# A state-space layer and a long convolution on one core: the parameter rows issued from one queue, and the first blocks' small work in another order

## The chip, the cores and the metric

The kernel runs on one core of a Trainium2 chip. The metric is the device time of one execution in microseconds (us). The kernel before took 198.16 us (median of three runs, 197.69 to 199.36).

## The reference, cut to what matters

Two independent layers work on 2048 rows of 640 channels in bf16, and their outputs are joined along the channels.

```
# A: diagonal complex state space, P = D = 640
dt = exp(log_dt);  Lam_bar = exp(dt * Lam);  B_bar = ((Lam_bar - 1) / Lam)[:, None] * Bmat
Bu = einsum("bld,pd->blp", x, B_bar)
h_t = Lam_bar * h_{t-1} + Bu_t                     # 2048 steps
y_A = 2 * Re(einsum("blp,dp->bld", h, Cmat)) + x * Dskip
# B: shift, gate and a causal convolution of full length, per channel
kv  = (4-tap filter of k by shift_k) * v
y_B = q * (causal_conv(kv, ssm_k) + kv * ssm_D)    # by FFT of length 4096
out = concatenate([y_A, y_B], axis=-1)
```

## The kernel before, in words

Layer A treats the 2048 steps as 512 groups of four; `s` (0 to 3) is the place in the group and `j` (0 to 4) one of five blocks of 128 states. `pe_in` (L515, items `v{s}_{j}`) multiplies x by B for one block and one place: 10 matmuls of 128x512, and for s other than 1 four more that add the place before, multiplied by diagonal matrices of Lam_bar (`diagL`, items `dL0` to `dL2`). The order within a block is s = 1, 2, 3, 0, and each waits for the eviction `ve` of the one before. `dve_rot`, `dve_scan`, `dve_back` and `dve_out` then run the recurrence over the 512 groups on VectorE, and `pe_proj` (items `p{i}_{s}`) multiplies by C. Layer B takes five groups of 128 channels: `pe_tap` does the short filter, `pe_s1`, `pe_s2`, `pe_inv` and `pe_fin` the transform in two factors and back.

Every piece of work is an item of a plan (`make_plan`) with a name and a function, and the string `ORDER` (L942) lists the items. Items are recorded in this order, so it is the program order of each engine and each DMA queue; engines run beside each other and wait for each other by semaphores. `@0` to `@6` is the PSUM tile that an item uses (`@0` ps0, `@2` ps1, `@4` ps2, `@6` ps3), and `!` takes the item's second engine (for an eviction VectorE instead of ScalarE; for a load of a parameter row SyncE's queue instead of ScalarE's).

The items of the first 30 us that matter here:

- `lv0` to `lv4` (L171) load log_dt, Lambda_im, Lambda_re, Dskip and ssm_D, five rows of 128 each, and `lsk` (L174) loads shift_k, all into the tile `As_h`. `B0`, `B1` (L178) load two blocks of B (two DMAs each, re and im); `x1`, `x2`, `x3`, `x0` (L184) load x transposed, 128x5x512 each.
- `wm0` to `wm4` (L325) are matmuls on the identity whose results nobody uses. `tsk` (L345, 12 small matmuls) transposes shift_k, `tske` (L349) copies it out to `sk_b`. `tv` (L329) transposes the parameter rows, `tve` (L334 to L336) copies them to `vec` and `vecb`. `bt0`, `bt1` (L487) transpose the two blocks of B, `be0!` (VectorE, L467) and `be1` (ScalarE, L469) copy them to `BT`.
- From `vec`: `exp` (L353), `rho` (L357, L358), `Fi` (L363 to L368), `rr` (L371), `trig1` (sine and cosine, L375, L165, L166), `lam` (L382 to L385), `dL` (L388 into `diagL`), `gam` (L425 to L433), `dG` (L388, three into the tile `H`: `diagG` lies there). `den` (L415 to L418) is a reciprocal that only `gam` needs.
- `dS0` (L638) builds the diagonals of the short filter for group 0, `dD` (L388 into `diagD`) those of Dskip, `drhs`, `dcm` and `dcol` (L250, L255, L258) spread ssm_D. `kS0` (L627) copies the swapped halves of k, `tap0_0` and `tap0_1` (L650) are the first filter matmuls, `bg` (L501) and `bge` the scaled blocks of B and their evictions, `kv0_0`, `kv0_1` (L655) the product with v.

The DMAs share eight counting semaphores in turn. A DMA that takes up one again has a wait on it: it is issued only when the one that had it before has landed. In the order listings these are the waits `DMAHW0` to `DMAHW7`.

Of the kernel before, what the change touches and what calls it, by code (L numbers as in the profile page):

```python
# [939 lines left out]


ORDER = """  # L942
lv1! pc lsk lv0! lv4 B0 pc2 dc dc3 wm0@0 lv2 zer lv3 pc3 dc2 wm1@2 B1 gp1 dsel x1 tsk@4 gp0 bt0@6 tske@4 dS0 tv@0 wm2@2 pp tve@0
bt1@4 x2 pk den exp wm3@0 be1@4 rho Fi wm4@2 rr be0!@6 v1_1@0 tp0 dD trig1 prr drhs G1 lam tp1 v1_0@2 x3 dL1 pow ve1_1@0 dL2 dL0
tab0 dcm@4 gam v2_1@6 gp3 aRM vT0 ve1_0!@2 tab1 tp2 dcol@4 dG B3 v2_0@0 G3 kT0 tp3 ve2_1!@6 tab2 dRM v3_1@2 ve2_0!@0 tab3 tp4 B4
x0 v3_0@4 tab4 ve3_1!@2 hp0 kS0 G0 hp1 bg1@6 ve3_0!@4 B2 H0 bg2@0 gp2 CT0 bge1!@6 tap0_0@2 H1 tap0_1@4 hp2 kv0_0@2 v0_0@6
kv0_1@4 bge2@0 hp3 H2 dS1 hs0 kvo0 bg3@2 H3 ve0_0!@6 kT1 v0_1@0 rs0 bge3@2 ca0 sc0 bg0@4 ve0_1@0 v1_3@6 bge0@4 ve1_3@6 had0
s1h0_2@2 s1he0_2@2 s1h0_0@0 s1he0_0@0 qi0 ra0 rout0 rs1 sc1 ra1 rout1 kS1 kvs0 v1_2@4 ve1_2@4 oa2_0 v1_4@6 s1h0_3@2 s1h0_1@0
s1he0_3@2 s1he0_1@0 ve1_4@6 vT1 v2_2@4 ve2_2@4 s1k0_2@2 s1k0_1@0 tap1_1@6 s1k0_3@4 s1ke0_2!@2 s1ke0_1@0 s1ke0_3@4 s1k0_0@2
# [95 lines left out]
```

## Time and profile before

| | |
|---|---|
| median of three runs | 198.16 us |
| the profiled execution, its span | 197.26 us, 195.5 us |
| busy, share of the span | PE 183.3 us (94%), VectorE 174.9 (89%), ScalarE 145.9 (75%), GpSimd 24.7 (13%) |
| DMA | mean 173 GB/s, its engines busy in nearly every slice after the first |
| granted TensorE clock | 0.998 |

PE is TensorE's matmul side and PEld its weight loads; DVE is VectorE, ACT ScalarE, POOL GpSimd, SPq and ACTq the DMA issues of SyncE and ScalarE. A row of the timeline gives the start, the duration from the first start to the last end, engine, line, operation, output and inputs, the count, and in brackets the engine's idle time just before and what ended it. PE works for nearly the whole span; its busy time counts matmuls that overlap, so it is not PE at its peak.

### The profile page before, as it was taken

How to read it: one execution, taken by the hardware profiler on the slowest of the kernel's cores; microseconds unless marked ns; L12 is line 12 of the kernel's file. 1: busy time of each engine (PE TensorE's matmuls, PEld its weight loads, DVE VectorE, ACT ScalarE, POOL GpSimd, SP SyncE). 2: the span in 40 equal slices, each digit the busy share in tenths (PEclk: the TensorE clock that was granted, in tenths of full speed). 3: DMA queues.
4: the chain of work that ended last, by engine and by line, in shares of the span. 5: the costliest groups of instructions: out<-in, count | busy, mean ns of one | idle time of the engine just before them, and what ended most of it. 6: DMA issues, size and time to landing. Idle time of an engine off the chain costs nothing.

```text
span 195.5 us, 7462 instructions
## 1 busy us (share of the span) xinstructions
PE 183.3 (94%) x3304; PEld 125.5 (64%) x3304; DVE 174.9 (89%) x302; ACT 145.9 (75%) x179; POOL 24.7 (13%) x55
## 2 busy tenths in 40 slices
PE   7799999999999999999988889999899999999991
PEld 4444365544565455785668666888688877977770
DVE  5899877999999999998999999999888989899571
ACT  2499999976978898899989997798768874710100
POOL 8899562000000000000000000000000000000000
PEclk9999999999999999999999999999999999999999
DMA  4999999999999919869599999997991999198763
GB/s 119 199 223 195 179 216 207 195 212 169 195 207 149 163 22 257 172 95 172 160 161 124 182 176 231 192 170 163 166 223 38 188 157 326 32 199 186 212 170 104
DMA packets 126061, 33.75 MB, mean 173 GB/s; under 512 B 121032, under 2 KB 125389, under 8 KB 126029
## 3 DMA queue, kind: packets, MB, share of 16 engines
q1 hardware_dynamic: 125988, 33.27, 89.5%
q8 instruction: 26, 0.43, 0.9%
q14 instruction: 7, 0.05, 0.1%
q10 hardware_dynamic: 40, 0.01, 0.0%
HBM read 10.66 MB, written 7.86 MB: 95 GB/s over the span
## 4 chain that ended last, share of the span: by engine, by line
PE 65%; DVE 14%; ACT 13%; issue 3%; DMA 2%; POOL 0%; ACTq 0%; DVEq 0%; POOLq 0%
PE ps L584 23%; PE ps L522 13%; PE ps L679 6%; PE ps L666 4%; DMA h_st<-in_B_ssm_k_dram 2%; ACT Xs L469 2%; ACT kS L625 2%; ACT zz L469 2%; PE ps L705 2%; PE ps L524 2%; ACT As_h L469 2%; ACT Hf L469 2%; PE ps L525 2%; PE ps L708 2%; PE ps L706 2%
## 5 line engine op out<-in xcount | busy, mean ns | idle before, releaser
L522 PE MATMUL ps<-xT,BT 128*128 128x512 bf16 x200 | 48.5, 379 | 1.3 <-DMA xT<-in_A_x_dram 1.2
L584 PE MATMUL ps<-Cs,hs 128*128 128x320 bf16 x240 | 35.9, 299 | 0.7 <-issue 0.5
L522 PEld LDWEIGHTS <-BT 128*128 128x128 bf16 x200 | 18.7, 98 | 23.5 <-issue 1.5
L584 PEld LDWEIGHTS <-hs 128*128 128x128 bf16 x240 | 22.3, 98 | 8.9 <-issue 0.9
L469 ACT CAST BT<-ps 128x640 bf16<-128x640 f32 (+3 forms) x13 | 9.4, 726 | 17.9 <-PE ps L589 17.9
L679 PEld LDWEIGHTS <-G 128*64 128x64 bf16 x640 | 18.9, 110 | 4.4 <-issue 3.1
L469 ACT CAST As_h<-ps 128x1024 bf16<-128x1024 f32 x20 | 20.0, 1036 | 2.1 <-PE ps L666 2.1
L469 ACT CAST Hf<-ps 128x1024 bf16<-128x1024 f32 x20 | 20.0, 1028 | 1.4 <-PE ps L679 1.4
L469 ACT CAST As_kv<-ps 128x1024 bf16<-128x1024 f32 x19 | 18.8, 1023 | 2.4 <-PE ps L666 2.4
L469 ACT CAST Xs<-ps 128x1024 bf16<-128x1024 f32 x19 | 19.3, 1039 | 1.0 <-PE ps L679 1.0
L469 ACT CAST zz<-ps 128x1024 bf16<-128x1024 f32 x18 | 17.9, 1031 | 1.3 <-PE ps L708 1.0
L705 PE MATMUL ps<-Xs,H 128*128 128x128 bf16 x80 | 17.6, 220 | 0.0
L708 PE MATMUL ps<-Xs,H 128*128 128x128 bf16 x80 | 17.5, 219 | 0.0
L706 PE MATMUL ps<-Xs,H 128*128 128x128 bf16 x80 | 17.5, 219 | 0.0
L707 PE MATMUL ps<-Xs,H 128*128 128x128 bf16 x80 | 17.5, 219 | 0.0
L729 DVE TENSOR_TENSOR qb<-ps,qb 128x1024 bf16<-128x1024 f32 x10 | 12.1, 1222 | 3.6 <-PE ps L724 3.3
L691 DVE TENSOR_TENSOR rot<-Xs,Hf 128x2048 bf16<-128x2048 bf16 x10 | 12.2, 1222 | 1.2 <-ACT Xs L469 0.6
L697 DVE TENSOR_TENSOR Xs<-Xs,rot 128x1024 bf16<-128x1024 bf16 x20 | 12.9, 686 | 0.2
L655 DVE TENSOR_TENSOR vT<-ps,vT 128x1024 bf16<-128x1024 f32 x10 | 11.8, 1217 | 1.1 <-ACT h L469 0.7
L692 DVE TENSOR_TENSOR Xs<-Xs,Hf 128x2048 bf16<-128x2048 bf16 x10 | 12.2, 1225 | 0.5
L679 PE MATMUL ps<-As_kv,G 128*64 128x128 bf16 x320 | 11.9, 220 | 0.6 <-DVE vT L655 0.4
L679 PE MATMUL ps<-As_h,G 128*64 128x128 bf16 x320 | 11.6, 221 | 0.1
(205 smaller groups left out, 391.5 us busy)
## 6 DMA issues: line engine op xcount, KB each, us to landing
h_st<-in_B_ssm_k_dram SPq DMA_DIRECT2D x10, 256.0 KB, 4.4
kv_rows<-vT SPq DMA_DIRECT2D x5, 512.0 KB
qb<-in_B_q_dram SPq DMA_DIRECT2D x5, 512.0 KB
kv_st<-kv_rows SPq DMA_DIRECT2D x10, 256.0 KB, 4.7
out_dram<-qb SPq DMA_DIRECT2D x5, 512.0 KB, 5.0
out_dram<-BT SPq DMA_DIRECT2D x15, 160.0 KB, 3.2
BT<-in_A_x_dram SPq DMA_DIRECT2D x6, 160.0 KB, 4.5
As_kv<-in_A_B_re_dram SPq DMA_DIRECT2D x3, 160.0 KB, 2.3
```

Source lines behind the costliest of these rows:

```text
L469: self.nc.scalar.copy(out=out, in_=in_)
L522: mm(o, lhsT=self.BT[:, r, k, j * 128:(j + 1) * 128], rhs=xT[:, k, :], start=(k == 0), stop=(s == 1 and k == NT - 1))
L584: mm(o[:, 0:320], lhsT=h[:, r, ts], rhs=self.Cs[:, r, j, c0:c0 + 320], start=(j == 0 and r == 0), stop=(not on_pe and j == NT - 1 and r == 1))
L679: self.nc.tensor.matmul(o[64 * e:64 * e + 64, c:c + 128], lhsT=self.G[:, r, k, :], rhs=As[:, k, :], start=True, stop=True)
L691: tt(out=self.cross(), in0=X[:, ::-1, :], in1=self.Hf[:, 1:2, hs].to_broadcast([128, 2, 1024]), op=ALU.mult)
L692: tt(out=X, in0=X, in1=self.Hf[:, 0:1, hs].to_broadcast([128, 2, 1024]), op=ALU.mult)
L697: self.nc.vector.tensor_tensor(out=X[:, r, :], in0=X[:, r, :], in1=cr[:, r, :], op=ALU.add if r else ALU.subtract)
L705: mm(o_re, lhsT=self.H[:, 0, k1, :], rhs=yre, start=True, stop=False)
L706: mm(o_re, lhsT=self.H[:, 2, k1, :], rhs=yim, start=False, stop=True)
L707: mm(o_im, lhsT=self.H[:, 1, k1, :], rhs=yre, start=True, stop=False)
L708: mm(o_im, lhsT=self.H[:, 0, k1, :], rhs=yim, start=False, stop=True)
L729: self.nc.vector.tensor_tensor(out=self.qb[:, :, cs].rearrange("p a (i c) -> p a i c", c=4), in0=ps[:].rearrange("p a n -> p (a n)").rearr ...
```

## The change

Only the string `ORDER` is changed, in its first four lines; all functions and all durations of single instructions stay.

```
-lv1! pc lsk lv0! lv4 B0 pc2 dc dc3 wm0@0 lv2 zer lv3 pc3 dc2 wm1@2 B1 gp1 dsel x1 tsk@4 gp0 bt0@6 tske@4 dS0 tv@0 wm2@2 pp tve@0
-bt1@4 x2 pk den exp wm3@0 be1@4 rho Fi wm4@2 rr be0!@6 v1_1@0 tp0 dD trig1 prr drhs G1 lam tp1 v1_0@2 x3 dL1 pow ve1_1@0 dL2 dL0
-tab0 dcm@4 gam v2_1@6 gp3 aRM vT0 ve1_0!@2 tab1 tp2 dcol@4 dG B3 v2_0@0 G3 kT0 tp3 ve2_1!@6 tab2 dRM v3_1@2 ve2_0!@0 tab3 tp4 B4
+pc lv4 B0 lv0 pc2 dc lv1 dc3 wm0@0 lv2 B1 zer lv3 pc3 lsk dc2 wm1@2 x1 gp1 dsel bt0@6 wm2@2 gp0 tv@0 tve@0 pp exp rho bt1@4 rr
+Fi tsk@2 be0!@6 x2 pk be1@4 wm3@0 tske@2 drhs trig1 den wm4@2 tp0 prr lam v1_1@0 dL1 dL2 dL0 G1 tp1 v1_0@2 x3 pow ve1_1@0 gam
+tab0 dcm@4 v2_1@6 gp3 aRM vT0 ve1_0!@2 tab1 tp2 ve2_1!@6 dcol@4 dG B3 v2_0@0 G3 kT0 tp3 tab2 ve2_0!@0 dRM dS0 dD v3_1@2 tab3 tp4
```

(The fourth line differs only by a shift of one word.) What this does to the engines stands in the listings below; `[waits ...]` names the semaphore that an instruction waits for, with the engine or the DMA semaphore that counts it up.

On ScalarE, the very start; first the order before. `As_h` holds all parameter rows.

```order
L174 DMA As_h<-in_B_shift_k_dram 5x512
L171 DMA As_h<-in_B_ssm_D_dram 5x128
L171 DMA As_h<-in_A_Lambda_re_dram 5x128
L171 DMA As_h<-in_A_Dskip_dram 5x128
L353 ACT_TABLE_LOAD
L353 ACTIVATE dt_b<-vec 128x5 [waits DVE_49]
L469 COPY BT<-ps_66 128x10x128 [waits PE_49]
L371 ACTIVATE rr<-rho 128x5 [waits DVE_49]
```

And the same place after the change:

```order
L171 DMA As_h<-in_B_ssm_D_dram 5x128
L171 DMA As_h<-in_A_log_dt_dram 5x128
L171 DMA As_h<-in_A_Lambda_im_dram 5x128
L171 DMA As_h<-in_A_Lambda_re_dram 5x128
L171 DMA As_h<-in_A_Dskip_dram 5x128 [waits DMAHW0_49]
L174 DMA As_h<-in_B_shift_k_dram 5x512 [waits DMAHW2_49]
L353 ACT_TABLE_LOAD
L353 ACTIVATE dt_b<-vec 128x5 [waits DVE_49]
L371 ACTIVATE rr<-rho 128x5 [waits DVE_49]
L469 COPY BT<-ps_66 128x10x128 [waits PE_49]
```

ScalarE now issues six loads instead of four, the last two behind a wait for an earlier load's landing, and `rr` stands ahead of the eviction `be1`. SyncE's queue loses its first two DMAs and begins with B0.

On PE, the last two warm-up items and the first matmul of `v1_1` (spaces: unchanged; - before, + after). Ahead of this piece, `tsk` has gone from the place before `bt0` to the place behind `bt1`, and now writes ps1 (`ps_65`).

```order
 L325 MATMUL ps_64<-ident 128x512
 L325 LDWEIGHTS ident
-L325 MATMUL ps_65<-ident 128x512
+L325 MATMUL ps_65<-ident 128x512 [waits DVE_49]
 L325 LDWEIGHTS ident
 L325 MATMUL ps_65<-ident 128x512
 L522 LDWEIGHTS BT [waits Activation_49]
-L522 MATMUL ps_64<-xT_136,BT 128x512 [waits DMAHW2_49]
+L522 MATMUL ps_64<-xT_136,BT 128x512 [waits DMAHW1_49]
```

The warm-up `wm4` writes the tile that `tsk` has just filled, so it now waits for VectorE's copy of it (`sk_b`, L349), and `v1_1` stands behind it.

On VectorE, from the end of `gam` on, first before (`hs_140` and `hs_142` are the states of blocks 0 and 1, `h_143` those of block 1 at s = 3):

```order
L467 CAST hs_140<-ps_65 128x1024 [waits PE_49]
L258 CAST dcol_b<-ps_66 128x160 [waits PE_49]
L388 TENSOR_TENSOR H<-ident,gamb 128x384 [waits DVE_49]
L388 TENSOR_TENSOR H<-ident,gamb 128x384 x2
L467 CAST hs_142<-ps_67 128x1024 [waits PE_49]
L284 TENSOR_TENSOR R<-r_cv,r_mask 128x128 [waits Activation_49]
L287 SCALAR_TENSOR_TENSOR Mq<-m_cv,m_mask 128x64 [waits Activation_49]
L467 CAST hs_140<-ps_64 128x1024 [waits PE_49]
L467 CAST h_143<-ps_65 128x2x512 [waits PE_49]
```

and after:

```order
L467 CAST hs_140<-ps_65 128x1024 [waits PE_49]
L467 CAST hs_142<-ps_67 128x1024 [waits PE_49]
L258 CAST dcol_b<-ps_66 128x160
L388 TENSOR_TENSOR H<-ident,gamb 128x384 [waits DVE_49]
L388 TENSOR_TENSOR H<-ident,gamb 128x384 x2
L467 CAST hs_140<-ps_64 128x1024 [waits PE_49,Activation_49]
L284 TENSOR_TENSOR R<-r_cv,r_mask 128x128 [waits Activation_49]
L287 SCALAR_TENSOR_TENSOR Mq<-m_cv,m_mask 128x64 [waits Activation_49]
L638 TENSOR_TENSOR diagS<-id_70,sk_b 128x512
L388 TENSOR_TENSOR diagD<-ident,vecb 128x640
L467 CAST h_143<-ps_65 128x2x512 [waits PE_49]
```

The eviction `ve2_1!` (`hs_142`) moves ahead of `dcol` and `dG`, `ve2_0!` ahead of `dRM`, and `dS0` and `dD` come from the first 11 us to the place before `ve3_1!`. Earlier on VectorE, `den` goes from the place ahead of `rho` to the place ahead of `lam`, and `tske` behind `be0!`. GpSimd's order is the same.

More of the change, by code (lines that the diff above doesn't have):

```diff
@@ L942 @@
 ORDER = """
-lv1! pc lsk lv0! lv4 B0 pc2 dc dc3 wm0@0 lv2 zer lv3 pc3 dc2 wm1@2 B1 gp1 dsel x1 tsk@4 gp0 bt0@6 tske@4 dS0 tv@0 wm2@2 pp tve@0
-bt1@4 x2 pk den exp wm3@0 be1@4 rho Fi wm4@2 rr be0!@6 v1_1@0 tp0 dD trig1 prr drhs G1 lam tp1 v1_0@2 x3 dL1 pow ve1_1@0 dL2 dL0
-tab0 dcm@4 gam v2_1@6 gp3 aRM vT0 ve1_0!@2 tab1 tp2 dcol@4 dG B3 v2_0@0 G3 kT0 tp3 ve2_1!@6 tab2 dRM v3_1@2 ve2_0!@0 tab3 tp4 B4
-x0 v3_0@4 tab4 ve3_1!@2 hp0 kS0 G0 hp1 bg1@6 ve3_0!@4 B2 H0 bg2@0 gp2 CT0 bge1!@6 tap0_0@2 H1 tap0_1@4 hp2 kv0_0@2 v0_0@6
+pc lv4 B0 lv0 pc2 dc lv1 dc3 wm0@0 lv2 B1 zer lv3 pc3 lsk dc2 wm1@2 x1 gp1 dsel bt0@6 wm2@2 gp0 tv@0 tve@0 pp exp rho bt1@4 rr
+Fi tsk@2 be0!@6 x2 pk be1@4 wm3@0 tske@2 drhs trig1 den wm4@2 tp0 prr lam v1_1@0 dL1 dL2 dL0 G1 tp1 v1_0@2 x3 pow ve1_1@0 gam
+tab0 dcm@4 v2_1@6 gp3 aRM vT0 ve1_0!@2 tab1 tp2 ve2_1!@6 dcol@4 dG B3 v2_0@0 G3 kT0 tp3 tab2 ve2_0!@0 dRM dS0 dD v3_1@2 tab3 tp4
+B4 x0 v3_0@4 tab4 ve3_1!@2 hp0 kS0 G0 hp1 bg1@6 ve3_0!@4 B2 H0 bg2@0 gp2 CT0 bge1!@6 tap0_0@2 H1 tap0_1@4 hp2 kv0_0@2 v0_0@6
 kv0_1@4 bge2@0 hp3 H2 dS1 hs0 kvo0 bg3@2 H3 ve0_0!@6 kT1 v0_1@0 rs0 bge3@2 ca0 sc0 bg0@4 ve0_1@0 v1_3@6 bge0@4 ve1_3@6 had0
```

## The prediction

> **What bounds the kernel now.** I read the page, then busy time by stretches, the waits of the first 30 us, and the timeline of that part.
>
> ```profile
> 9.60:26.60 17.00, 16.60 (x77) 7.50 (x77) 15.41 (x31) 16.66 (x33) 13.10 (x21) 1.00 1.06 202
> 33.60:60.00 26.40, 26.20 (x477) 14.65 (x475) 25.92 (x42) 21.26 (x26) 0.00 (x0) 1.00 1.08 187
> 90.00:120.00 30.00, 26.38 (x822) 19.84 (x824) 28.75 (x38) 28.27 (x32) 0.00 (x0) 1.00 1.01 174
> 9.59 4.48 PE L522 MATMUL ps<-xT,BT 128*128 128x512 bf16 x20 [1.24 <-DMA xT<-in_A_x_dram]
> 21.66 0.38 PE L524 MATMUL ps<-hs,diagL 128*128 128x512 bf16 x1 [0.40 <-DVE hs L467]
> ```
>
> Behind each stretch stand its length, then busy us of PE, PEld, DVE, ACT and POOL, the clock, the DMA share and GB/s. PE is the bound: from 9.6 us on it hardly rests, and between 33.6 and 60 us DVE is as full. The two PE rows show, in brackets, its only marked waits between warm-up and 30 us: 1.24 us until the first transposed x has landed, and 0.40 us for an eviction by VectorE. What the change does to these two is what it can do for PE. The first in detail:
>
> ```profile
> 0.72 0.39 SPq L171 DMA_DIRECT2D As_h<-in_A_Lambda_im_dram  x1
> 1.48 0.36 SPq L178 DMA_DIRECT2D As_kv<-in_A_B_re_dram  x1
> 2.36 0.46 SPq L178 DMA_DIRECT2D As_kv<-in_A_B_re_dram  x1
> 3.34 9.85 SPq L184 DMA_TRANSPOSE xT<-in_A_x_dram  x3
> DMA to landing us min/median/max: 2.3/2.4/2.5
> ```
>
> SyncE spends its first 0.76 us (0.72 to 1.48) on two parameter rows, then issues B0, B1 and x1; x1 goes out at 3.34, and v1_1 begins at 9.59, when it has landed. The last row is B0's and B1's time to landing.
>
> **The change part by part.** *SyncE.* Without the two rows B0 goes out at 0.72. Four issues of B at the same pace would end at 3.34 - 0.76 = 2.58, but x1 now waits for the semaphore of B0's first half, which lands 2.3 to 2.5 us after its issue, at 3.0 to 3.2. So x1 goes out about 0.25 us earlier, not 0.76, and lands at about 9.3. If its landing hung on the bytes ahead of it alone, it would be 8.8; if on nothing that moved, 9.59. I take 9.3, since the wait stands in the order.
>
> *ScalarE's queue.* lv4, lv0, lv1 and lv2 go out from 0.7 on, at the 0.38 us a piece of SyncE's two until 2.2. Dskip's row then waits for lv4's landing. How long such a small load takes is bounded by the issue at 2.36 above: it waits for shift_k's load, which ScalarE issued first of all, and follows its neighbour without a gap, so that load needed at most some 1.7 us. Dskip's row goes out by 2.4, shift_k by about 3.0. With B's 2.5 us to landing they are there by 4.9 and 5.5; the table load behind them ends before 5.
>
> *PE up to v1_1.*
>
> ```profile
> 3.17 1.16 PE L345 MATMUL ps<-ident,As_h 5*128 5x5 bf16 x12
> 5.43 0.10 PEld L329 LDWEIGHTS <-As_h 25*128 25x128 bf16 x1 [0.20 <-DMA As_kv<-in_A_B_im_dram]
> 5.57 1.03 PE L325 MATMUL ps<-ident 128*128 128x512 bf16 x2
> 5.88 0.47 DVE L336 TENSOR_SCALAR vec<-vec 128x3 f32<-128x3 f32 x1
> 5.10 1.23 POOL L294 TENSOR_TENSOR Hf<-Hf,gs 128x512 int32<-128x512 int32 x1
> 6.39 0.17 DVE L415 TENSOR_TENSOR pq<-vec 128x10 f32<-128x10 f32 x1
> 7.27 0.16 DVE L357 CAST dtf<-dt_b 128x5 f32<-128x5 bf16 x1
> 8.79 0.82 DVE L467 COPY BT<-ps 128x1280 bf16<-128x1280 bf16 x1
> 4.37 0.34 DVE L349 CAST sk_b<-ps 128x40 bf16<-128x40 f32 x1 [0.81 <-PE ps L345]
> ```
>
> Ahead of tv, tsk goes out (1.1 us) and wm2 comes in (0.8 us of starts), so tv runs about 0.25 earlier, at 5.2, provided Dskip's row is there (4.9). That gains nothing by itself: L336 took 0.47 us for 15 numbers, to 6.35, and GpSimd's L294 ended at 6.33. GpSimd's order is unchanged, so I let L336 end there again.
>
> What gains is that den no longer stands ahead of rho: L357 follows at 6.39 instead of 7.27, 0.88 earlier, and Fi and be0 with it. be0 runs from 7.9 to 8.7, sk_b (0.34) to 9.05. Here the change adds a wait: wm4 may not overwrite ps1 before sk_b is copied. Behind tv stand bt1, tsk and wm3, some 2.6 us, so PE is through at about 8 and rests; behind wm4 stands v1_1. Two matmuls at the warm pace of 0.215 us (below) after 9.05, v1_1 starts at 9.48. x1's landing (9.3) and be1 (8.1, next paragraph) are earlier. **So the first wait shrinks by only 0.11 us**: a DMA's wait is replaced by one on a small copy of VectorE's.
>
> *The parameter chain.*
>
> ```profile
> 7.52 1.23 ACT L469 COPY BT<-ps 128x1280 bf16<-128x1280 bf16 x1 [1.43 <-PE ps L487]
> 8.88 1.28 ACT L375 ACT_TABLE_LOAD   x1
> 10.84 0.20 DVE L382 TENSOR_TENSOR lam<-rr,cos 128x5 f32<-128x5 f32 x1
> ```
>
> rr goes ahead of be1, which follows bt1's end (6.6) at 6.9 and ends at 8.1; the second table load then ends at 9.4, and sine and cosine (before, 0.68 from the load's end to lam) at 10.1. On VectorE drhs and den (0.88) follow sk_b and end at 10.2. lam starts 0.6 earlier. Its instructions meet GpSimd's table products, which come only 0.5 earlier, so I let dL and gam be 0.5 earlier. PE did not wait for them and does not now.
>
> *The eviction.*
>
> ```profile
> 18.51 1.24 PE L522 MATMUL ps<-xT,BT 128*128 128x512 bf16 x5
> 19.59 0.38 PE L524 MATMUL ps<-hs,diagL 128*128 128x512 bf16 x1
> 20.02 1.24 PE L522 MATMUL ps<-xT,BT 128*128 128x512 bf16 x5
> 17.24 3.24 DVE L388 TENSOR_TENSOR H<-ident,gamb 128x384 bf16<-128x384 bf16 x3
> 20.40 1.21 DVE L467 CAST hs<-ps 128x1024 bf16<-128x1024 f32 x1
> ```
>
> Five matmuls and the next start are normally 1.08 us apart (18.51 to 19.59); from 20.02 to the row at 21.66 it is 1.64, so the wait costs 0.56 us of starts. v2_1 had ended seven starts of 0.215 ahead of 18.51, at 17.0, yet its eviction ran at 20.40, behind dG's 3.24 us. After the change it stands ahead of dG, runs from 16.9 to 18.1, and v3_1 asks for it at about 21.0. **This 0.56 us is gained whole.** dG is late instead; PE needs it only for bg1, shortly ahead of tap0_0 (28.50).
>
> *What VectorE pays.* sk_b and dS0 leave a time when it idled (0.81 us ahead of sk_b alone), and dS0 and dD now stand ahead of ve3_1, kS0, ve3_0, bge1 and kv0.
>
> ```profile
> 4.74 0.69 DVE L638 TENSOR_TENSOR diagS<-id,sk_b 128x512 bf16<-128x512 bf16 x1
> 9.52 1.16 DVE L388 TENSOR_TENSOR diagD<-ident,vecb 128x640 bf16<-128x640 bf16 x1
> 23.80 1.23 DVE L467 CAST h<-ps 128x1024 bf16<-128x1024 f32 x1 [0.69 <-PE ps L525]
> 25.06 0.97 DVE L627 COPY kS<-kT 64x1032 bf16<-64x1032 bf16 x2
> 26.82 1.23 DVE L467 CAST h<-ps 128x1024 bf16<-128x1024 f32 x1 [0.79 <-PE ps L525]
> 28.50 0.40 PE L650 MATMUL ps<-kT,diagS 64*64 64x512 bf16 x1
> 29.61 2.36 DVE L655 TENSOR_TENSOR vT<-ps,vT 128x1024 bf16<-128x1024 f32 x2 [0.43 <-PE ps L650]
> 30.36 1.25 PE L522 MATMUL ps<-xT,BT 128*128 128x512 bf16 x5
> 33.60 1.23 DVE L467 CAST z<-ps 128x1024 bf16<-128x1024 f32 x1 [1.03 <-PE ps L525]
> ```
>
> They add 0.69 + 1.16 = 1.85 us; ahead of the two evictions VectorE idled 0.69 + 0.79 = 1.48, and 0.5 comes from its earlier start. Step by step: ve2_1 ends at 18.1, dcol 18.3, dG 21.5, ve2_0 22.7, dRM 23.2, dS0 and dD 25.0, ve3_1 26.2, kS0 27.2, ve3_0 28.4, bge1 29.6. PE, 0.67 earlier, wants kS0 for tap0_0 at 28.50 - 0.67 = 27.8 and the tile that bge1 frees for v0_0 at 30.36 - 0.67 = 29.7. Both are met, the second with 0.1 us to spare. dG's price is the open one: at 3 x 0.69 = 2.07 (diagS's row, of more elements) VectorE would be 1.2 us earlier. I take 3.24, as it was.
>
> [...]
>
> *The sum.* 0.11 + 0.56 = 0.67 us by 33.6 us. There VectorE had waited 1.03 us for PE, so both are earlier from then on, and both are full to 60 us. DMA does not move with them: kv0 begins at 29.6 as before, and its store with it. But the first load that hangs on it has room:
>
> ```profile
> L631 SPq DMA_DIRECT2D kv_st<-kv_rows x2: 1682/2002/2322, 39.4 to 41.1; - x2
> DMA to landing us min/median/max: 6.5/6.5/6.5
> 49.07 0.71 PE L666 MATMUL ps<-R,kv_st 64*64 64x64 bf16 x64
> ```
>
> Its second half goes out at 41.1, lands at 47.6 and is read at 49.07: 1.5 us of room for 0.67. So the profiled execution goes from 197.26 to 196.6 us, and the median of the runs shown, 0.90 above it, from 198.16 to **197.5 us**.
>
> **The rivals.** *The gain is given back.* Between 90 and 120 us PE rests 3.6 us while VectorE and ScalarE are busy 28.75 and 28.27 of 30: a head start of 0.67 may be spent there on another order of arrivals. For it: that stretch, and DMA's clock that stays; against: the three engines come to it earlier together. Time: 198.2.
>
> *VectorE becomes the bound at 25 us* (the slower side). If dS0 and dD cost what dG does, 1.08 us per 384 elements, they take 1.44 + 1.80 = 3.24 instead of 1.85, 1.4 more. With 0.1 us to spare at bge1, v0_0 starts 1.3 late: 198.16 - 0.67 + 1.3 = 198.8. It decides from the point where bge1 ends after 29.7. For it: dG's row; against: the rows of diagS and diagD themselves.
>
> *The parameter rows come too late.* ScalarE's waits put Dskip's row behind another load's landing, and tv waits for all five rows. If the issue at 2.4 took twice B's 2.4 us, for all of B is under way by then, it would land at 7.2, and L336, some 0.6 behind tv, would end at about 7.8 instead of 6.35; sk_b, wm4 and v1_1 follow 1.4 later: 198.16 - 0.67 + 1.4 = 198.9. Against: four loads of B at once took 2.3 to 2.5.
>
> *More than forecast.* If dG falls to 2.07 VectorE never holds PE up, and if Fi and be0 are quicker v1_1 starts on x1's landing at 9.3: 0.85 gained, 197.3, inside the forecast's own range.
>
> **How the numbers follow.** Forecast, with the dearer gain: 0.53, own range 197.0 to 198.0. Given back: 0.22. VectorE late: 0.16. Rows late: 0.09. The range 196.4 to 199.4 takes in the forecast and the rivals, with 0.5 us beyond the slowest of them and 0.6 beyond the forecast's own range for what the later stretches make of a shift, and for the scatter of the runs shown. About 1% (196.2 to 200.1) is what a measurement here can tell from no change. Faster by over 1% needs 2 us, three times the sum: 0.07, from a better meeting of the engines at 90 to 120 us. Slower by over 1% is the tail of the two slower rivals: 0.13. Within: 0.80.
>
> **What would show it.** v1_1 at 9.4 to 9.6 us, released by wm4 and no longer by x1; L357 at 6.4; no wait of PE at the L524 near 21 us; ve2_1 at 17; bge1's end at 29.6 or earlier, v0_0 at 29.7; VectorE's eviction of v0_0 at about 32.9 instead of 33.60. Wrong would be tv after 5.5 us, a wait of PE for kS0 or bge1 before 31 us, or a shift of 0.6 us at 33 us that the end does not show.

## The result

| | before | after |
|---|---|---|
| median of 20 executions each | 198.06 us (197.09 to 199.37) | 197.28 us (195.37 to 198.93) |
| ratio after / before, 95% interval | | 0.9948 (0.9926 to 0.9971) |
| the profiled execution, its span | 197.26, 195.5 us | 195.37, 193.6 us |

The change gains about half a per cent, 0.8 us by the medians; 0.67 us was forecast. The profiled execution is 1.9 us faster, and it is not a typical one. The kernel after has two kinds of executions, told apart by the mean granted clock beside each time. Over all its 33 executions of this study, 14 with a mean clock of 0.997 to 1.0 have a median of 196.13 us, and 19 with 0.978 to 0.991 one of 197.56. The kernel before was at 0.995 or above in all 70 executions of it that ran beside the experiments (median 197.74); in its first profile what is missing to 1.0 lies at the very end (0.94 from 190 to 195.5 us). So the change gains 1.6 us in one kind and 0.2 in the other. That is pooled: in the first 20 executions it was 2.0 and 0.5 us (196.07 and 197.53 against 198.06), and in the 12 of e5 the one kind gained 1.3 and the other lost 0.9 (196.19 and 198.33 against 197.47). The forecast lies between by luck as much as by its working. The prediction held a difference under 1% to be hard to tell here; with 20 executions of each, half a per cent could be told. (The ratios here and below leave out executions over 1.5% above the fastest of their kernel, which drops some of the slower kind, three of twelve in e5 and two of six in e7; so I count both kinds over all executions.)

Below are rows of the kernel after, in its first profiled execution: DMA issues, weight load, PE and VectorE, with the same columns as before (start, duration, engine, line, operation, count, idle time just before and what ended it).

```profile
3.00 2.88 SPq L184 DMA_TRANSPOSE xT<-in_A_x_dram  x1
5.29 0.10 PEld L329 LDWEIGHTS <-As_h 25*128 25x128 bf16 x1 [0.84 <-DMA As_h<-in_A_Dskip_dram]
6.07 0.16 DVE L357 CAST dtf<-dt_b 128x5 f32<-128x5 bf16 x1
8.21 0.32 DVE L349 CAST sk_b<-ps 128x40 bf16<-128x40 f32 x1
8.59 0.59 PE L325 MATMUL ps<-ident 128*128 128x512 bf16 x2 [0.33 <-DVE sk_b L349]
9.02 4.48 PE L522 MATMUL ps<-xT,BT 128*128 128x512 bf16 x19
16.62 1.23 DVE L467 CAST hs<-ps 128x1024 bf16<-128x1024 f32 x1 [0.44 <-PE ps L525]
18.00 1.88 DVE L388 TENSOR_TENSOR H<-ident,gamb 128x384 bf16<-128x384 bf16 x3
19.44 1.24 PE L522 MATMUL ps<-xT,BT 128*128 128x512 bf16 x5
20.52 0.38 PE L524 MATMUL ps<-hs,diagL 128*128 128x512 bf16 x1
32.46 1.23 DVE L467 CAST z<-ps 128x1024 bf16<-128x1024 f32 x1 [1.03 <-PE ps L525]
```

v1_1 begins at 9.02 behind wm4, which waits for sk_b; no wait is left at the L524 of block 1 (20.52 is 1.08 behind 19.44, the normal distance); VectorE takes v0_0's eviction at 32.46 instead of 33.60. Two more profiles of the same kernel, taken later, show how much of this changes from one execution to the next; first the second profile (clock 1.0), then the third (0.991):

```profile
8.60 0.59 PE L325 MATMUL ps<-ident 128*128 128x512 bf16 x2 [0.49 <-DVE sk_b L349]
9.59 3.18 PE L522 MATMUL ps<-xT,BT 128*128 128x512 bf16 x13 [0.41 <-DMA xT<-in_A_x_dram]
18.57 1.49 DVE L388 TENSOR_TENSOR H<-ident,gamb 128x384 bf16<-128x384 bf16 x3
29.80 1.25 PE L522 MATMUL ps<-xT,BT 128*128 128x512 bf16 x4
```

```profile
5.99 0.18 PE L329 MATMUL ps<-ident,As_h 25*128 25x25 bf16 x1 [1.09 <-DMA As_h<-in_A_Dskip_dram]
9.31 1.01 PE L325 MATMUL ps<-ident 128*128 128x512 bf16 x2 [0.42 <-DVE sk_b L349]
10.12 5.07 PE L522 MATMUL ps<-xT,BT 128*128 128x512 bf16 x20
30.92 1.25 PE L522 MATMUL ps<-xT,BT 128*128 128x512 bf16 x5
6.80:8.50 1.70, 1.70 (x15) 0.82 1.04 214
8.50:10.20 1.70, 1.28 (x4) 0.50 0.98 165
10.20:11.90 1.70, 1.70 (x7) 0.68 0.98 221
```

v1_1 starts at 9.02, 9.59 and 10.12, released by wm4, by x1's landing, and by wm4 again, late because Dskip's row was late. In the third profile the last three rows (windows of PE: length, busy time and count, clock, DMA share, GB/s) show TensorE's clock at half. If the clock was whole or half at each moment, a stretch at half clock takes half of its length off the mean, and what is missing to 1.0 counts twice: from these windows I estimate 2 x 1.7 x (0.18 + 0.50 + 0.32) = 3.4 us at half clock. The 20 matmuls that take 4.48 us otherwise take 5.07.

One table holds the rest together. For each profiled execution: v1_1's start, the time from the first to the end of the 20 matmuls of v1_1 and v1_0, v0_0's start, and v0_0 minus v1_1 minus what the 20 matmuls took beyond 4.48. The experiments are described below.

| kernel | v1_1 | 20 matmuls | v0_0 | path |
|---|---|---|---|---|
| before, two profiles | 9.59, 9.48 | 4.48, 4.48 | 30.36, 30.63 | **20.77, 21.15** |
| after, three profiles | 9.02, 9.59, 10.12 | 4.48, 4.48, 5.07 | 29.22, 29.80, 30.92 | 20.20, 20.21, 20.21 |
| e1, evictions alone | 9.16 | 4.68 | 29.66 | 20.30 |
| e2, one eviction back | 9.36 | 4.48 | 30.42 | **21.06** |
| e3, rows on SyncE | 9.93 | 5.25 | 30.91 | 20.21 |
| e4, wm4 without a wait | 8.94 | 5.42 | 30.09 | 20.21 |
| e6, wm3 of five | 10.66 | 4.61 | 30.99 | 20.20 |
| e7, no wait, wm3 of four | 9.95 | 4.48 | 30.15 | 20.20 |
| e8, before without wm3 and wm4 | 10.09 | 7.38 | 33.20 | 20.21 |
| e9, den early | 10.50 | 6.29 | 32.52 | 20.21 |
| e10, wm4 of five | 9.67 | 4.48 | 29.88 | 20.21 |

With both evictions moved, v0_0 is v1_1 plus 20.2 us plus what the clock cost. Without the move it is later by what VectorE makes PE wait; in e8, which has the old order too, PE was so late that VectorE no longer held it up. From v0_0 to the product at L691 near 94 us pass 64.23 to 64.26 us wherever at least `ve2_0` was moved, and 64.55 to 64.58 in the two profiles of before and in e8; the rest, to the last L603, scatters between 95.8 and 97.0 us in all kernels alike.

### The profile page after: what moved, and what is told of

Its sections match the earlier page's. It is cut to its first block, busy times and chain, and to the rows that moved or that the text cites. A ratio compares the mean times of both kernels' runs of the same rounds, so it can differ in the third digit from the quotient of the medians.

```text
span 193.6 us, 7451 instructions
## 1 busy us (share of the span) xinstructions
PE 182.7 (94%) x3291; PEld 125.4 (65%) x3304; DVE 173.8 (90%) x302; ACT 145.7 (75%) x179; POOL 23.9 (12%) x55
## 3 DMA queue, kind: packets, MB, share of 16 engines
HBM read 10.66 MB, written 7.86 MB: 96 GB/s over the span
## 4 chain that ended last, share of the span: by engine, by line
PE 71%; ACT 13%; DVE 10%; issue 4%; POOL 0%; ACTq 0%; POOLq 0%; DVEq 0%
PE ps L584 23%; PE ps L522 18%; PE ps L679 6%; PE ps L666 4%; ACT Xs L469 2%; PE ps L524 2%; PE ps L525 2%; ACT kS L625 2%; ACT zz L469 2%; PE ps L705 2%; ACT As_h L469 2%; ACT Hf L469 2%; PE ps L708 2%; PE ps L706 2%; PE ps L707 2%
## 5 line engine op out<-in xcount | busy, mean ns | idle before, releaser
L522 PE MATMUL ps<-xT,BT 128*128 128x512 bf16 x187 | 47.5, 379 | 1.1 <-ACT Xs L469 0.2
L691 DVE TENSOR_TENSOR rot<-Xs,Hf 128x2048 bf16<-128x2048 bf16 x10 | 12.2, 1222 | 1.1 <-ACT Xs L469 0.5
L655 DVE TENSOR_TENSOR vT<-ps,vT 128x1024 bf16<-128x1024 f32 x10 | 11.9, 1219 | 0.8 <-PE ps L650 0.4
L679 PE MATMUL ps<-As_kv,G 128*64 128x128 bf16 x320 | 11.9, 220 | 0.3 <-ACT zz L469 0.3
```

The lines of the kernel that those rows point to most:

```text
L522: mm(o, lhsT=self.BT[:, r, k, j * 128:(j + 1) * 128], rhs=xT[:, k, :], start=(k == 0), stop=(s == 1 and k == NT - 1))
L679: self.nc.tensor.matmul(o[64 * e:64 * e + 64, c:c + 128], lhsT=self.G[:, r, k, :], rhs=As[:, k, :], start=True, stop=True)
L691: tt(out=self.cross(), in0=X[:, ::-1, :], in1=self.Hf[:, 1:2, hs].to_broadcast([128, 2, 1024]), op=ALU.mult)
```

## The experiments

The first four ran together (before: median 197.72), as did the next four (197.47) and the last four (197.96).

**e1: the evictions alone.** The kernel before, with one line of ORDER changed:

```
-tab1 tp2 dcol@4 dG B3 v2_0@0 G3 kT0 tp3 ve2_1!@6 tab2 dRM v3_1@2 ve2_0!@0 tab3
+tab1 tp2 ve2_1!@6 dcol@4 dG B3 v2_0@0 G3 kT0 tp3 tab2 ve2_0!@0 dRM v3_1@2 tab3
```

> The order before with one thing of the change alone: the evictions ve2_1 and ve2_0 ahead of dG and dRM. Loads, den, tsk, dS0 and dD stay where they were. Theory (two gains that add: 0.57 us from v1_1's earlier start, 0.56 from this eviction): v1_1 starts at 9.59 as before, PE's step of 1.64 us before the L524 near 21.66 becomes 1.08, and PE is 0.56 earlier from there to the end: 197.5 against 198.06, ratio 0.997. Rival (only the earlier start pays; the eviction's wait moves to another place): PE waits as long somewhere else by 34 us and the ratio is 1.000.

Measured: 196.52 us, ratio 0.993 (0.9902 to 0.9959); the clock at 0.996 or above in all nine executions. This edit alone is worth as much as the whole change (0.9948), as far as the intervals tell, and about twice the 0.56 us that was expected of it (1.2 us by the medians).

```profile
9.16 1.66 PE L522 MATMUL ps<-xT,BT 128*128 128x512 bf16 x6
29.66 1.25 PE L522 MATMUL ps<-xT,BT 128*128 128x512 bf16 x4
91.59 2.39 DVE L655 TENSOR_TENSOR vT<-ps,vT 128x1024 bf16<-128x1024 f32 x2 [0.34 <-ACT h L469]
```

The third row's product in the first profile of the kernel before:

```profile
92.67 2.35 DVE L655 TENSOR_TENSOR vT<-ps,vT 128x1024 bf16<-128x1024 f32 x2 [0.70 <-ACT h L469]
```

The path of e1 (20.30) is 0.47 us shorter than in the first profile of before. The product at 92 us is a gain that no term had: VectorE waits 0.34 us there instead of 0.70. The two make 0.8 of the 1.2 us; the rest is within the interval. Up to v1_1 the order of e1 is that of before, so its start at 9.16 instead of 9.59 is scatter.

**e2: one eviction back.** The change, with `ve2_1` behind `dcol` and `dG` again:

```
-tab1 tp2 ve2_1!@6 dcol@4 dG B3 v2_0@0 G3 kT0 tp3 tab2
+tab1 tp2 dcol@4 dG B3 v2_0@0 G3 kT0 tp3 ve2_1!@6 tab2
```

> The changed order with ve2_1 put back behind dcol and dG; all else as changed. Theory of two gains that add: v1_1 at 9.0 as after, but v3_1's L524 waits again: dG, which runs from about 16.5 under two GpSimd products, costs up to 3.2 us, ve2_1 ends between 19.6 and 20.9 and PE, which asks for it at 20.5, loses 0 to 0.56 us; ratio against before 0.996 to 0.998. Rival (the wait was there only because VectorE was late in the order before): ve2_1 is done by 20.5, no wait, ratio 0.995 as after.

Measured: 197.28 us, ratio 0.9966 (0.9941 to 0.9991). The time is the one that the theory of two gains gave, but it came about another way.

```profile
16.35 3.23 DVE L388 TENSOR_TENSOR H<-ident,gamb 128x384 bf16<-128x384 bf16 x3
16.50 1.35 POOL L457 TENSOR_TENSOR qb<-Xs,Fi 128x512 int32<-128x512 int32 x1
17.82 1.35 POOL L457 TENSOR_TENSOR kv_st<-Xs,Fi 128x512 int32<-128x512 int32 x1
29.16 1.21 DVE L467 CAST BT<-ps 128x1024 bf16<-128x1024 f32 x1
29.29 0.37 PE L650 MATMUL ps<-kT,diagS 64*64 64x512 bf16 x1 [0.23 <-DVE h L467]
30.42 1.24 PE L522 MATMUL ps<-xT,BT 128*128 128x512 bf16 x4
```

PE no longer waits at L524, since VectorE is earlier than in the kernel before. It waits later instead: dG takes 3.23 us beside two GpSimd products (1.35 us each; the same two take 1.04 in the first two profiles of the change), `dS0` and `dD` stand behind it, dRM's first product and kS0 meet further GpSimd products (1.09 and 1.63 us, 0.28 and 0.88 in the change), tap0_1 waits for `ve3_0`'s eviction (the row at 29.29), and bge1 ends at 30.4. v0_0 follows at 30.42, as late as in the kernel before (30.36). This is the rival of VectorE as the bound at 25 us, and moving `ve2_1` out from behind dG is what keeps it away in the change: there dG runs when GpSimd's products are nearly done and takes 1.88 or 1.49 us.

**e3: the rows back on SyncE.** The change, with `lv1` and `lv0` first on SyncE's queue again:

```
-pc lv4 B0 lv0 pc2 dc lv1 dc3
+lv1! pc lv0! lv4 B0 pc2 dc dc3
```

> The changed order with the two rows Lambda_im and log_dt again first on SyncE's queue; all else as changed, shift_k still the last load of ScalarE. Theory (x1's landing and sk_b's copy are almost level after the change, so both must be early): x1 goes out at 3.34 and lands at 9.5, PE waits for it again, v1_1 starts at 9.5 to 9.6, 0.55 later than after, and the end with it: ratio against before 0.997 to 0.998. Rival (the queue is worth nothing since v1_1 hangs on sk_b and wm4): v1_1 at 9.0 to 9.1, ratio 0.995 as after.

Measured: 198.08 us, ratio 0.9991 (0.9963 to 1.0018): no gain is left that can be measured.

```profile
3.81 1.25 PE L487 MATMUL ps<-ident,As_kv 128*128 128x128 bf16 x10 [0.58 <-DMA As_kv<-in_A_B_re_dram]
9.93 5.25 PE L522 MATMUL ps<-xT,BT 128*128 128x512 bf16 x19
```

PE has no wait for x1 here, so it had landed in time. What is late is B0: bt0 waits for it, everything of PE behind it is about 0.6 later, and with the clock still at half pace (5.25 for the 20 matmuls) v1_1 begins at 9.93. With tsk moved away, bt0 is the first thing that PE can do after wm1, and it needs B0 early. So, as I read it, the move of tsk needs the move of the rows. The mean clock of this execution is 0.999, so it does not show the slow start (see e8).

**e4: wm4 without its wait.** The change, with wm4 on tile ps0, where nothing is to be copied out first:

```
-Fi tsk@2 be0!@6 x2 pk be1@4 wm3@0 tske@2 drhs trig1 den wm4@2 tp0 prr lam v1_1@0
+Fi tsk@2 be0!@6 x2 pk be1@4 wm3@0 tske@2 drhs trig1 den wm4@0 tp0 prr lam v1_1@0
```

> The changed order with one PSUM tile changed: wm4 writes ps0 instead of ps1, so it no longer waits for VectorE's copy of sk_b. Theory (in the changed kernel v1_1 starts at 9.02 because of wm4's wait, while x1 has landed by about 8.5): wm4 follows wm3 at 8.1, v1_1 starts at 8.5 to 8.6 on x1's landing, 0.45 earlier, and the end with it: ratio against before 0.992 to 0.993. Rival (x1's landing is what sets v1_1 already): v1_1 stays at 9.0, ratio 0.995.

Measured: 196.26 us, ratio 0.9893 (0.9857 to 0.9929), one of six executions at 0.991. This was the one that was profiled:

```profile
4.09 0.59 PE L325 MATMUL ps<-ident 128*128 128x512 bf16 x2
7.31 1.77 PE L325 MATMUL ps<-ident 128*128 128x512 bf16 x4
8.94 5.42 PE L522 MATMUL ps<-xT,BT 128*128 128x512 bf16 x19
6.80:8.50 1.70, 1.70 (x12) 0.70 0.79 177
8.50:10.20 1.70, 1.70 (x6) 0.50 1.18 251
10.20:11.90 1.70, 1.65 (x7) 0.80 0.96 166
```

Again, by the same estimate, 2 x 1.7 x (0.30 + 0.50 + 0.20) = 3.4 us at half clock. In this profile wm2 already ran at the full pace (the first row: 0.59 us for two matmuls, 1.06 in the first two profiles of the change), so the clock had risen by about 4.1 us, and by the first window it fell again at about 7.5 (8.5 - 2 x 1.7 x 0.30, an estimate). In between PE had rested 0.65 us in one piece (for B1's imaginary half) and had run bt1 and tsk, whose matmuls are 128x128 and 5x5. So v1_1 came at 8.94 and not at the 8.5 to 8.6 that was expected. This made the clock the theory for the second four. An early rise alone is not enough for a fall: in e2's profile wm2 took 0.59 us too, at 4.74, and its mean clock is 1.0.

**e5: the change again**, unchanged.

> The changed kernel itself, again, beside the three others. Its 20 executions so far fall into two heaps: at a mean granted clock of 1.0 they took 195.4 to 196.3 us, at 0.991 they took 196.8 to 198.0. The kernel before was never at 0.991. Theory A (clock): the rest of PE ahead of wm4, and the light matmuls of tsk before it, let TensorE's clock fall back to half for one stretch of about 3.5 us (195 x 0.009 x 2) in about half of all executions, which costs 1.3 us each time; expected again: about half at 0.991, these 1.2 to 1.6 us slower than the rest, median 196.8 to 197.5, ratio about 0.995. Theory B (scatter of DMA landings alone): times scatter by 1 us without regard to the clock.

Measured: 196.4 us over its 12 executions, ratio 0.9935 (0.9908 to 0.9963). Five of the twelve were at 0.990 or 0.991 and took 197.0 to 198.4 us, the other seven 195.2 to 196.4 without overlap. The times follow the clock, as theory A said. The profiled execution is one at 1.0; its rows stand above as the second profile.

**e6: three more matmuls in wm3**, ahead of the wait, so that PE doesn't rest there. The five pairs are the counts of wm0 to wm4, each with the item that it follows.

```
-((2, "dc"), (2, "wm0"), (2, "bt0"), (2, "bt1"), (2, "wm3"))
+((2, "dc"), (2, "wm0"), (2, "bt0"), (5, "bt1"), (2, "wm3"))
```

> The change, with five warm-up matmuls in wm3 instead of two (three more of 128x512 on the identity, 0.65 us warm or 1.3 us cold); wm4 still waits for sk_b's copy. They fill the time in which PE rested ahead of wm4, and add nothing to what v1_1 waits for when the clock is warm. Theory A (clock): the clock no longer falls back, or in far fewer executions; median 195.8 to 196.4, ratio about 0.990. Theory B (the wait for sk_b is what costs): the wait is the same, ratio 0.995 as the change has it. If neither, three more cold matmuls ahead of v1_1 cost 0.6 to 1.3 us: ratio 0.998 to 1.001.

Measured: 195.77 us, ratio 0.9913 (0.9885 to 0.9942), none of six below 0.996. If the 19 of 33 in the unchanged kernel were spread at random over both, six without one would come about once in 80 times; against e5 alone, which ran beside it with five of twelve, once in eleven. The rows show the price in an execution where the clock rose late:

```profile
7.70 3.17 PE L325 MATMUL ps<-ident 128*128 128x512 bf16 x7
10.66 2.02 PE L522 MATMUL ps<-xT,BT 128*128 128x512 bf16 x7
```

Seven matmuls at 0.43 us instead of four hold v1_1 up to 10.66. This execution took 196.89 us, the slowest of the six, and still less than the median of the kernel before.

**e7: both.** wm4 on ps0, four matmuls in wm3.

```
-tske@2 drhs trig1 den wm4@2 tp0
+tske@2 drhs trig1 den wm4@0 tp0
-((2, "dc"), (2, "wm0"), (2, "bt0"), (2, "bt1"), (2, "wm3"))
+((2, "dc"), (2, "wm0"), (2, "bt0"), (4, "bt1"), (2, "wm3"))
```

> The change with wm4 on tile ps0, so that it waits for nothing of VectorE's, and four matmuls in wm3 instead of two. PE then has no rest between tsk and the landing of x1 at 8.5 to 9.5 us. Theory A (clock): no or few executions at 0.991; v1_1 at about 9.0 to 9.3, on x1's landing; median 195.6 to 196.2, ratio 0.988 to 0.991, as wm4 on ps0 alone gave in its better executions. Theory B (no clock, only the wait): the same as wm4 on ps0 alone, 0.989, with the same share of executions at 0.991.

Measured: 196.11 us, ratio 0.9896 (0.9862 to 0.9931), one of six at 0.991 (198.22 us) and one at 0.996 that was as slow (198.72). The better four took 194.9 to 196.8. The ratio rests on those four. It is not better than e4; six executions don't tell the two apart.

```profile
6.69 1.47 PE L325 MATMUL ps<-ident 128*128 128x512 bf16 x6
9.95 2.75 PE L522 MATMUL ps<-xT,BT 128*128 128x512 bf16 x11 [1.79 <-DMA xT<-in_A_x_dram]
```

Here PE rests 1.79 us for x1, which released it at 9.95, and the clock does not fall (its mean is 1.0). So a rest alone is not enough.

**e8: the kernel before without wm3 and wm4**; both issue nothing.

```
-((2, "dc"), (2, "wm0"), (2, "bt0"), (2, "bt1"), (2, "wm3"))
+((2, "dc"), (2, "wm0"), (2, "bt0"), (0, "bt1"), (0, "wm3"))
```

> The kernel before without the last two warm-up items: wm3 and wm4 issue no matmul (six on the identity are left instead of ten). Nothing waits for them, so by the waits alone v1_1 starts on x1's landing at 9.6 us as before. Theory A (clock): PE now rests from 7.3 us on for over 2 us, so the clock falls back in many executions, which the kernel before never showed: a share of them at 0.991 or lower and 1.3 us slower, median 198.2 to 199.2, ratio 1.003 to 1.008. Theory B (no clock): ratio 1.000.

Measured: 198.48 us as the median of its 12 executions, 1.0 above before (1.005, in the range of theory A), but the ratio is 1.0018 (0.9994 to 1.0043), below that range, and no execution was below 0.995. So the mean clock shows no fall here. In the profiled execution the clock hadn't risen when v1_1 began:

```profile
10.09 2.72 PE L522 MATMUL ps<-xT,BT 128*128 128x512 bf16 x6 [2.39 <-DMA xT<-in_A_x_dram]
10.20:11.90 1.70, 1.70 (x5) 1.00 1.67 223
33.20 1.25 PE L522 MATMUL ps<-xT,BT 128*128 128x512 bf16 x4
```

Six matmuls take 2.72 us, 0.43 a start, while the clock column says 1.00. In this trace the column does not show the half pace ahead of a first rise; only the distance of the matmuls does. So the mean clock, my mark for this experiment, counts falls alone: a slow start costs time too, and it does not see it. The profiled execution (200.45 us) is the slowest of the twelve; its 20 matmuls of v1_1 and v1_0 took 7.38 us.

**e9: den early.** The change, with den back ahead of exp and rho:

```
-dc2 wm1@2 x1 gp1 dsel bt0@6 wm2@2 gp0 tv@0 tve@0 pp exp rho bt1@4 rr
-Fi tsk@2 be0!@6 x2 pk be1@4 wm3@0 tske@2 drhs trig1 den wm4@2
+dc2 wm1@2 x1 gp1 dsel bt0@6 wm2@2 gp0 tv@0 tve@0 pp den exp rho bt1@4 rr
+Fi tsk@2 be0!@6 x2 pk be1@4 wm3@0 tske@2 drhs trig1 wm4@2
```

> The change with den alone put back ahead of exp and rho on VectorE. My prediction took den's move as what brings L357 forward by 0.88 us. Theory A (the chain to sk_b is on PE's path): L357 at 6.9 to 7.3, sk_b's copy about 0.8 later, at 9.0; wm4 and with it v1_1 at 9.4 to 9.7 instead of 9.0 to 9.6, PE's rest ahead of wm4 1.1 to 1.3 us instead of 0.3 to 0.5; the path from v1_1 to v0_0 stays at 20.21 us; 0.2 to 0.4 us slower than the change, ratio 0.995 to 0.997, and the clock falls back in as many executions as in the change (half) or more. Theory B (x1's landing at 8.5 to 9.9 is the path, sk_b is hidden behind it): no difference from the change, 0.9935 to 0.995.

Measured: 199.07 us, ratio 1.0058 (1.0036 to 1.0081), 2.2 us slower than the change by the ratios and slower than before. This is the largest effect of all: the direction of theory A, at more than five times its size.

```profile
7.07 0.16 DVE L357 CAST dtf<-dt_b 128x5 f32<-128x5 bf16 x1
9.31 0.33 DVE L349 CAST sk_b<-ps 128x40 bf16<-128x40 f32 x1
9.70 1.01 PE L325 MATMUL ps<-ident 128*128 128x512 bf16 x2 [1.12 <-DVE sk_b L349]
10.50 6.29 PE L522 MATMUL ps<-xT,BT 128*128 128x512 bf16 x20
```

L357 is 1.0 us later and sk_b's copy 1.1, about as expected of theory A. PE rests 1.12 us ahead of wm4, v1_1 starts at 10.50 with no wait for x1 in its row, and then the matmuls run at half pace for so long that the 20 take 1.81 us more. This execution's mean clock is 0.996, and all its warm-up matmuls ran at half pace too: it shows a late rise, not a fall. All ten executions took 198.4 to 199.6 us, seven of them at 0.991 or below. So the chain to sk_b is on PE's path, and being late there costs twice: once as the wait, and once more by the clock, which rises late or falls. In this change den's move is what pays for the new wait of wm4; alone it was not run.

**e10: the three matmuls behind the wait**, in wm4 instead of wm3.

```
-((2, "dc"), (2, "wm0"), (2, "bt0"), (2, "bt1"), (2, "wm3"))
+((2, "dc"), (2, "wm0"), (2, "bt0"), (2, "bt1"), (5, "wm3"))
```

> The change with the three additional warm-up matmuls not in wm3 but in wm4 (five instead of two), that is behind the wait for sk_b: PE works as much before x1 lands as with five in wm3, but rests ahead of wm4 as in the change. Theory A1 (the rest itself lets the clock fall): as many executions at 0.991 as the change has (18 of 32), median 197.3 to 197.9, ratio 0.996 to 0.999. Theory A2 (it is the work in the whole stretch that counts): none or few at 0.991, and v1_1 at 9.3 to 9.7: median 195.8 to 196.4, ratio 0.990 to 0.993, like five in wm3.

Measured: 196.87 us, ratio 0.995 (0.9914 to 0.9986), four of twelve at 0.990 or 0.991, between both theories; two at 0.996 took over 198 us as well. Against e6 it says that the place matters, but not with certainty (0 of 6 against 4 of 12).

**e11: the kernel before, a second profile.**

> A second profile of the kernel before. In all profiles so far the time from v0_0's first matmul (28 to 31 us) to the product with the twiddles at L691 near 74 us is 43.7 us, and from there to the next at 94 us 20.54 us, except 20.88 in the first profile of the kernel before. If that 0.35 belongs to the old order it is there again; if it is scatter, 20.54. From v1_1 to v0_0: 20.77 again (0.56 more than the 20.21 of every kernel with the eviction moved). x1 lands somewhere between 8.5 and 10 us.

```profile
9.48 3.18 PE L522 MATMUL ps<-xT,BT 128*128 128x512 bf16 x14 [0.21 <-DMA xT<-in_A_x_dram]
21.93 0.38 PE L524 MATMUL ps<-hs,diagL 128*128 128x512 bf16 x1 [0.78 <-DVE hs L467]
30.63 0.60 PE L522 MATMUL ps<-xT,BT 128*128 128x512 bf16 x2
92.92 2.36 DVE L655 TENSOR_TENSOR vT<-ps,vT 128x1024 bf16<-128x1024 f32 x2 [0.69 <-ACT h L469]
```

v1_1 starts 0.11 earlier than in the first profile, and PE waits 0.78 instead of 0.40 at L524; v0_0 is 0.27 later, and the path is 21.15, not the 20.77 that was expected. In the old order v0_0 hangs on VectorE's eviction, so there an earlier v1_1 is worth nothing. The wait of 0.7 us at 92 us is there again (0.69 in e8 too), and 0.32 to 0.34 in the change, in e1 and e2, and in every other profile with `ve2_0` moved. That gain of 0.35 comes with the evictions. The row names ScalarE's `h`, but that copy had ended 0.65 us before; what else releases the product there the runs do not show.

**e12: the change, a third profile.** Its rows stand above.

> A third profile of the changed kernel, to see where its clock falls when it does (18 of 32 executions). Theory A: with a mean clock of 0.991 the windows show a granted clock of 0.5 for about 3.5 us beginning at 7 to 8 us, v1_1's matmuls 0.43 us apart instead of 0.215 in that stretch, and v0_0 later by 0.9 to 1.4 us than v1_1's start + 20.21; without it, v0_0 is at v1_1 + 20.21.

It fell on an execution of the slower kind (197.33 us) and shows what theory A said: by the estimate above 3.4 us at half clock, from 7.9 to 11.3 us, and v0_0 at v1_1 + 20.21 + 0.59.

**The versions that beat both.** wm4 on a tile that nothing has to empty (e4) has 0.9893, three more idle matmuls in the rest (e6) 0.9913, each under the ratios of the change (0.9948 and 0.9935); the intervals still touch those of the change, so against it the gain is likely, not shown. By the plain medians of their runs the two are level (0.9926 and 0.9914).

## Why the prediction was right, and where it was not

**The eviction: right, and more than its sum.** The table gives 0.57 us for the forecast 0.56 (20.77 against 20.20), and the wait at L524 is gone. What the prediction did not see is that this wait is not a constant: it is VectorE's lateness against PE, 0.40 or 0.78 in two executions, and as long as it stood a gain ahead of it was swallowed, as far as two profiles tell. The second gain, 0.35 us at 92 us, was nowhere in the sum.

**v1_1's start: the step that failed.** The prediction put one number, 9.48, set by wm4, and a gain of 0.11. The runs show a maximum of two things that scatter: x1's landing (with the new queue it is issued at 2.92 to 3.07; it landed at 8.5, 5.5 us later, in the first profile after, and released PE at 9.95 in e7) and wm4. The earlier issue, which the prediction priced at 0.25 us, can't be told from the scatter: with the old queue, issued at 3.34 to 3.36, x1 released PE at 9.59, 9.48 and 10.09 (e8), and was there before 9.16 in e1. wm4 was earlier than forecast in two of three profiles (8.59 instead of 9.05). Most of it (L357 at 6.07 instead of 6.39) is because L336 no longer ended at 6.35; two rows of the first profile after:

```profile
5.74 0.42 DVE L336 TENSOR_SCALAR vec<-vec 128x3 f32<-128x3 f32 x1
5.09 1.04 POOL L294 TENSOR_TENSOR Hf<-Hf,gs 128x512 int32<-128x512 int32 x1
```

The prediction had let it end with GpSimd's L294 "there again"; L294 took 1.04 us instead of 1.23, and ended at 6.13. By the traces the difference is dS0, which ran beside it from 4.74 to 5.43 in the kernel before and has moved: L294 takes 1.23 us with dS0 there (before, e1) and 1.04 without (the change's three profiles, e2, e3, e4). It was not tried by itself.

**The clock: missing.** The prediction saw that PE would rest ahead of wm4 and priced the rest by its length alone. In 19 of 33 executions the mean clock (0.978 to 0.991) says that it fell, in most of them for some 3.5 us (2 x 195 x 0.009, an estimate that takes the fall to be to half, 0.50, as in the third profile), and these are 1.4 us slower by the medians. Why it falls the runs do not show. Ahead of the two falls that were profiled the longest rest of PE behind wm2 was 0.65 us (e4) and 1.09 us (third profile); in e7 it rested 1.79 us and the mean clock stayed at 1.0. That the new order invites the fall is argued, not shown apart. For it speaks that e3, whose bt0 is late, fell in 1 of 12, and e1, with the old order, in none of 9. An early rise goes with both profiled falls (wm2's two matmuls took 0.59 us in e4 and 0.77 in the third profile, against 1.06 in the first two); against it as the whole reason speak e2's profile (0.59) and e7's (0.75), both at a mean clock of 1.0.

**dG and VectorE: the alternative was right.** dG took 1.88, 1.49 and 1.49 us where 3.24 was taken and 2.07 stood as the other end; e2 shows dG and GpSimd's products both longer side by side (3.23, and 1.35 for 1.04). VectorE never held PE up at 25 us in the change: in the first profile bge1 ended at 28.05, 1.2 us ahead of v0_0, where 0.1 was forecast, and kv0, which the prediction left at 29.6, began at 28.48. Durations did change with the order, though, and not only downwards: `dD` took 1.66 us instead of 1.16, and drhs and den's L418 1.11 and 0.83 us beside GpSimd products (0.31 and 0.22 before). So lam came at 10.71 instead of 10.2. PE did not wait for it.

**The rivals.** The gain was not given back: 64.2 us from v0_0 to L691 at 94 us in every profile with the evictions moved, however early v0_0 was. VectorE as the bound is what e2 became. The parameter rows came late in one of three profiles, by 0.7 us (tv at 5.99, past the 5.5 that was to show the prediction wrong), not by the 1.4 of the rival; PE rested 1.09 us for them.

**The sum.** In executions of the first kind: 0.56 + 0.35 + 0.23 at v1_1 (the means of two profiles each, 9.54 and 9.31; with v1_1 between 9.16 and 10.09 in the four profiles with the old loads and tsk early, this last term is not shown) is 1.1 of the measured 1.6 us. The other 0.5 could be the wait at L524, which was 0.4 longer in the second profile of before, or the scatter behind 95 us; the profiles don't settle it. With 19 of 33 slower by 1.4 us, the gain on average is 1.6 - 0.8 = 0.8. The forecast 0.67 missed a gain of 0.9 and a loss of 0.8, which nearly cancel. Since e1 gains as much with the evictions alone, the intervals show no gain by the rest of the change (the queue, tsk, den).

## What to carry to other kernels

Parts of a reordering have no fixed price each: here the eviction had to move before an earlier start counted, and den had to move to pay for the new wait. Try each part alone: one of them may carry the whole gain. A short rest of PE in the first 10 us may cost more than its length: behind the 1.12 us in e9 the 20 matmuls took 1.81 us longer, and where e6 filled the rest, none of six executions was below 0.996. The mean clock beside each execution's time shows a fall before any trace does, though not a late rise, and one profile may show the rarer kind.

## What the runs showed of the hardware

- TensorE's granted clock read 0.50 from 8.5 to 10.2 us in e4 and in the third profile, and I estimate 3.4 us at half clock in each (from three windows of 1.7 us). In e7 PE rested 1.79 us and the mean clock stayed at 1.0. Why it falls in one and not in the other is not shown.
- The clock column read 1.00 from 10.2 to 11.9 us in e8 although the matmuls were still at half pace: 2.72 us for six of 128x512, against 1.46 for six at the full pace (the first six of v1_1 in the first profile after).
- The same transposing load of x, issued at 2.92 to 3.07 us, landed at 8.5 us in the first profile after and released PE at 9.59 in the second and at 9.95 in e7.
- VectorE's and GpSimd's products took longer beside each other (e2) than in the second profile after: 3.23 against 1.49 us for three of 128x384, and 1.35 against 1.04 for one of 128x512.
